# Attention, a cosine gate and a second expert in one kernel: the first two token blocks share the loading of the weights

## The chip, the cores and the metric

The kernel runs on one core of one Trainium2 chip, as a single launch. The metric is the device time of that launch in microseconds. Three runs of the kernel before took 1356.47, 1359.84 and 1358.34 us, so the median is 1358.34 us. A profiled execution, from which all rows below come, took 1353.98 us.

## The reference

Three stages follow each other. The first is an attention with pooled keys and values; its output is the input of a two-matrix stage with the gate h * cos(h); that output goes through a second two-matrix stage with a softmax-weighted gate and a layer norm. All arithmetic is float32.

```python
# q, k, v: (8, 8, 576, 64)
k_p = k.reshape(B, H, 72, 8, D).mean(axis=3)
v_p = v.reshape(B, H, 72, 8, D).mean(axis=3)
scores = scale * q @ k_p.T
attn = softmax(scores)
x = (attn @ v_p) -> (4608, 512)

h = x @ w_in                 # (4608, 2048)
y = (h * cos(h)) @ w_out     # (4608, 512)

h2 = y @ w2_in               # (4608, 1024)
solu = h2 * softmax(h2)
out = (layernorm(solu) * g_ln) @ w2_out
```

The matrices w_in, w_out, w2_in, w2_out arrive as float64 bits and are turned into float32 on the chip.

## The kernel before

The 4608 tokens are cut into 9 blocks of 512. The first part of the kernel, of which this document speaks, makes for every block the attention output x and from it h, in units. A unit is one block j and one pair q of 128-column chunks of w_in: 16 chunks make 8 pairs, so a block has 8 units and there are 72. A unit is 24 matmuls (`h_mm`, L608 to L622: two chunks, four row groups of x, and three products of high and low parts each) in 8 steps of three matmuls. The result stays in PSUM while a chain of four operations (`chain`, two on ScalarE (ACT), two on VectorE (DVE)) turns it into h * cos(h), which goes to DRAM. The later parts (y, and the second stage) read it from there, in an order of their own.

Around the units stand three kinds of other work, in an order that the program writes out by hand; each engine runs its own instructions in that order.

**Chunks of w_in.** Each of the 16 chunks is loaded as 64-bit words into a tile `raw` (L109, 512 KB), then goes through `s1` (ACT, L114 and L115), `bits` (DVE, L119, L123, L127), `join` (GpSimd (POOL), L139) and `c_in.done` (ACT L1100, POOL L1101), after which the chunk can be used in a matmul. The class `Pipe` moves three chunks at a time: each `pipe.step()` does bits and join of one chunk, the done of the one before and the s1 of the one after. Five steps stand before the units; in block 0 every unit has two more, at s = 1 and s = 5. Since ACT's s1 of a chunk takes a buffer that is freed by POOL's done of a chunk three earlier, the three engines go in step.

**Where chunks and other tiles lie.** Sixteen slots called `wi` hold the chunks for good. Before a chunk is there, a slot serves other tiles, given out in turn: slots 0 to 3 the raw keys of batch 0, 4 to 6 the v of batch 0 (`load_vn`), 7 to 9 the v of batch 1, 10 and 11 raw keys of batch 1, 12 the pooling matrix `pool_w`, 13 and 14 raw keys of batch 1. The raw words of chunks 6, 8, 10 and 12 to 15 are loaded into the chunk's own slot. So the load of chunk 8 goes into slot 8, which held the second tile of the v of batch 1, and the load of chunk 12 into that of `pool_w`; each must wait until the last pooling matmul that reads the old tile has run. All these loads and the loads of q (`load_q`, L379) stand in one queue, SP's, which issues in order.

**Attention of the next block.** For block 1 `Attn.plan` gives each piece a position, counted in steps of the units of block 0 (64 positions, 8 per unit): scores (`sc`, PE L391, then DVE L399 and L400, which free the PSUM tile), exponentials (ACT L457), `norm` (sums on DVE L476, scaling of the even heads of a pair on POOL and of the odd on DVE, L486 and L491), transposes (`eTp`, `eLp`, PE), their split in high and low parts (ACT, then DVE L527 and L510), and the products with v (`av`, PE L549, then ACT L551 and DVE L552), which write x. The score tiles, the transposes and the products all share two PSUM tiles, `ps_a`.

Block 0's attention stands before the units: keys of batch 0 are summed in groups of eight on DVE (L243, L245, L246), those of the other batches on POOL (L231, L251: `halves` and the last sum). The v of batches 0 and 1 is pooled by matmuls with `pool_w` (`pool_vn`, L287 and L290, two halves each) and brought into shape by `prep_vn` (DVE L301, L308, L317, ACT L314, L315, POOL L316).

Of the kernel before, what the change touches and what calls it, by code (L numbers as in the profile page):

```python
# [11 lines left out]
F32 = mybir.dt.float32  # L12
# [23 lines left out]
def fused_kernel(ctx, tc, qT_d, kT_d, vN_d, vM_d, vL_d, w_in, w_out, w2_in, w2_out, g_ln, out):  # L36
# [184 lines left out]
    def kv_jobs(b, hf):  # L221


        def raw_tile(n):
            if b < 2:
                return wi.tile([P, n], F32, "kvraw")
            return wo.tile([P, n], F32, "kvraw")

        def halves(x, n):
            for m in (4 * n, 2 * n):  # L230
                nc.gpsimd.tensor_tensor(out=x[:, 0:m], in0=x[:, 0:m], in1=x[:, m:2 * m], op=ALU.add)  # L231
            return x

        def k_job(i):
            p = 2 * hf + i
            raw = raw_tile(POOL * SP)
            nc.sync.dma_start(out=raw, in_=kT_d[b, p])
            dst = kT[b % 2][p]

            def add():  # L240
                if b == 0:
                    t = wo.tile([P, SP], F32, "kp")
                    nc.vector.tensor_reduce(  # L243
                        out=t, in_=raw.rearrange("p (r s) -> p s r", r=POOL), axis=AX.X, op=ALU.add)
                    nc.vector.tensor_copy(out=dst[0:D, 0:SP], in_=t[0:D])  # L245
                    nc.vector.tensor_copy(out=dst[D:P, SP:2 * SP], in_=t[D:P])  # L246
                else:
                    x = halves(raw, SP)
                    for a in range(2):
                        r = slice(D * a, D * (a + 1))  # L250
                        nc.gpsimd.tensor_tensor(  # L251
                            out=dst[r, SP * a:SP * (a + 1)], in0=x[r, 0:SP], in1=x[r, SP:2 * SP],
                            op=ALU.add)
            return add

        def v_job(i):
            if hf == 0 and i == 0:
                v_t[b] = ap1.tile([P, 6, D], F32, tag="v", name="v")
            dst = v_t[b][:, 2 * hf + i if i < 2 else 4 + hf]
            raw = raw_tile(POOL * D)  # L260
            nc.sync.dma_start(out=raw, in_=vM_d[b - 2, 2 * hf + i] if i < 2 else vL_d[b - 2, hf])

            def add():
                x = halves(raw, D)
                nc.gpsimd.tensor_tensor(out=dst, in0=x[:, 0:D], in1=x[:, D:2 * D], op=ALU.add)
            return add

        n = 3 if b >= 2 else 0
        return [lambda i=i: k_job(i) for i in range(2)] + [lambda i=i: v_job(i) for i in range(n)]
# [8 lines left out]
        nc.sync.dma_start(out=t[2][0:64, 0], in_=vN_d[b, 4, 0:64])  # L278

    def pool_vn(b, hf):  # L280
        if hf == 0:
            pool_vn.ps = ps_y.tile([P, 2, BLK], F32, tag="y", name="vps")
        main, left = pool_vn.ps[:, 0], pool_vn.ps[:, 1]
        t = v_t[b]
        c = slice(4 * D * hf, 4 * D * (hf + 1))
        for i in range(4):
            nc.tensor.matmul(  # L287
                main[:, c], lhsT=pool_w["m"][:, i], rhs=t[i // 2][:, i % 2, c], start=(i == 0),
                stop=(i == 3))
        nc.tensor.matmul(  # L290
            left[:, c], lhsT=pool_w["l"][0:64], rhs=t[2][0:64, 0, c], start=True, stop=True)
        v_t[b, hf] = main, left

    def prep_vn(b, hf):
        main, left = v_t.pop((b, hf))
        vm, vl = vM[b][:, hf], vL[b][:, hf]
        c = slice(4 * D * hf, 4 * D * (hf + 1))
        w = wo.tile([P, 4 * D], F32, "vw")
        u = wo.tile([P, 2, 4 * D], F32, "vu")
        hi = wo.tile([P, 4 * D], F32R, "vh")  # L300
        nc.vector.tensor_tensor(  # L301
            out=w.rearrange("p (i a d) -> p i a d", i=2, a=2),
            in0=main[:, c].rearrange("p (i a d) -> p i a d", i=2, a=2),
            in1=m_half.rearrange("p (o a u) -> p o a u", o=1, u=1).to_broadcast([P, 2, 2, D]),
            op=ALU.mult,
        )
        for k2, m in enumerate((m_head, m_hlo)):
            nc.vector.tensor_tensor(  # L308
                out=u[:, k2].rearrange("p (c d) -> p c d", c=4),
                in0=left[:, c].rearrange("p (c d) -> p c d", c=4),  # L310
                in1=m.rearrange("p (c o) -> p c o", o=1).to_broadcast([P, 4, D]), op=ALU.mult,
            )
        w = w.rearrange("p (i c) -> p i c", i=2)
        nc.scalar.copy(out=vm[:, 0], in_=w)  # L314
        nc.scalar.copy(out=hi, in_=u[:, 0])  # L315
        nc.gpsimd.tensor_tensor(out=vm[:, 1], in0=w, in1=vm[:, 0].bitcast(F32), op=ALU.subtract)  # L316
        nc.vector.scalar_tensor_tensor(  # L317
            out=vl.rearrange("p i c -> p (i c)"), in0=hi.bitcast(F32), scalar=m_sh, in1=u[:, 1],
            op0=ALU.mult, op1=ALU.add)

    def prep_v(b):
        src = v_t.pop(b)
# [34 lines left out]
    class Attn:  # L357
# [101 lines left out]
        def norm(self, *ps):  # L459
# [22 lines left out]
            def scale():  # L482
                for i, (p, e) in enumerate(zip(ps, es)):
                    i2 = p % 2
                    eng = nc.vector if self.j < 2 and i2 else nc.gpsimd
                    eng.tensor_tensor(  # L486
                        out=em[:, :, i2], in0=e[:, :, :, 0:KM],
                        in1=sv[:, i].to_broadcast([P, TPB, 2, KM]), op=ALU.mult,
                    )
                    for a in range(2):  # L490
                        eng.tensor_tensor(  # L491
                            out=el[:, :, 2 * i2 + a],
                            in0=e[:, :, a:a + 1, KM:SP].to_broadcast([P, TPB, 4, KL]),
                            in1=sv[:, i, :, a:a + 1].to_broadcast([P, TPB, 4, KL]), op=ALU.mult,
                        )
# [17 lines left out]

        def e_tr(self, p):
            hf, i2 = divmod(p, 2)
            tp = ps_a.tile([P, BLK], F32, tag="a", name="eTp")
            em = self.em[hf]
            eT = self.eT[p] = self.tile([P, 2, BLK], F32R, "eT")

# [39 lines left out]
        def plan(self, put):  # L559
# [29 lines left out]
            if self.j == 1:  # L589
                for i in range(2):  # L590
                    put(i, add, 1, 1, KV[i])
            for b in new:
                for i in range(6):
                    put(-10 + 2 * i, kv_load, b, i // 3, KV[2 + i % 3])
                    put(2 * i + i // 3, add, b, i // 3, KV[2 + i % 3])
# [4 lines left out]

    NQ = NF // 2
    units = [(j, q) for j in range(NB) for q in range(NQ)]
    yd = [dram.tile([P, KD, BLK], F32, tag="yd", name=f"yd{j}") for j in range(NB)]
    gd = [dram.tile([P, NQ, 2, BLK], F32, tag="gd", name=f"gd{j}") for j in range(NB)]
    w_in_t, w_op = [], [{} for _ in range(NQ)]
# [3 lines left out]
        return t.rearrange("p a b -> p (a b)")  # L609

    def h_mm(n, i, kk):
        j, q = units[n]
        if i == 0 and kk == 0:
            pool, tag = ((ps_q, "q"), (ps_y, "y"), (ps_y, "y"))[n % 3]
            h_ps[n] = pool.tile([P, 2, BLK], F32, tag=tag, name="h")
# [23 lines left out]
            h_ps.pop(n)  # L639

    def g_store(n):
        j, q = units[n]
        nc.sync.dma_start(out=gd[j][:, q], in_=h_t.pop(n))

    NH = BLK // 2
# [447 lines left out]
    def c_in(f):  # L1093
# [20 lines left out]
    with tc.manual_schedule():  # L1114
# [4 lines left out]
        for p in range(NPAIR):  # L1119
            kv_load(0, p // 2, KV[p % 2])  # L1120
            a0.load_q(p)
            if p == 1:
                order[0].load(raws[0])
        load_vn(0)
        for i in (1, 2, 3):
            order[i].load(raws[i])
# [44 lines left out]
        nc.scalar.activation(out=cst[:, 36:37], in_=halfpi, func=AF.Exp)  # L1171
        add(0, 0, "k0", "k1")
        a0.scores0(0)
        add(0, 1, "k0")
        a0.scores0(1)
        pipe.step()
        a0.now("norm", 0)
        add(0, 1, "k1")
        a0.scores0(2)
        a0.scores0(3)  # L1180
        a0.now("norm", 1)
        pipe.step()
        pool_vn(0, 0)
        pool_vn(0, 1)
        prep_vn(0, 0)
        a0.now("e_tr", 0)
        a0.now("norm", 2)
        a0.now("norm", 3)
        a0.now("e_tr_left", 0)
        a0.now("e_tr", 1)  # L1190
        prep_vn(0, 1)
        a0.now("av", 0)
        a0.now("e_tr", 2)
        add(1, 0, "k1")
        a0.now("av", 1)
        pipe.step()
        pool_vn(1, 0)
        a0.now("e_tr", 3)
        add(1, 0, "k0")
        a0.now("e_tr_left", 1)  # L1200
        prep_vn(1, 0)
        a0.now("av", 2)
        pool_vn(1, 1)
        pipe.step()
        prep_vn(1, 1)
        a0.now("av", 3)
        early = {7: raws[1], 9: raws[2], 11: raws[3]}
        pipe.todo += [(order[i], early.get(i)) for i in range(6, len(order))]
        pipe.step()
# [7 lines left out]
                work[BL * (j - 1) + pos].append(lambda: fn(*a))  # L1217
            return put

        for j in range(1, NB):  # L1220
            at[j].plan(put_at(j))
        last = len(units) - 1
        raws = [ap1.tile([P, BLK, 2], I32, tag=t, name="raw") for t in ("em", "eT")]
# [19 lines left out]
            put(50 + 7 * m, g_split, m)  # L1243
        put(62, g_load, 2)
        for n in range(len(units)):
            j, q = units[n]
            for s in range(SL):
                h_mm(n, s // KD, s % KD)
                if n > 1 and s == 3:
# [2 lines left out]
                    chain(n - 1, (0, 4, 7).index(s))  # L1252
                if n > 1 and s == 5:
                    g_store(n - 2)
                if j == 0 and s in (1, 5):
                    pipe.step()
                for fn in work[SL * n + s]:
                    fn()
# [200 lines left out]
```

## Time and profile before

| | us |
|---|---|
| three runs | 1356.47, 1359.84, 1358.34 |
| profiled execution | 1353.98 |
| its span | 1352.2 |
| PE busy | 1300.9 (96%) |
| DVE busy | 1059.3 (78%) |
| ACT busy | 697.7 (52%) |
| POOL busy | 499.8 (37%) |

The span is the time from the first to the last instruction; the execution's own time is 1.8 us longer. Shares are averages over stages: PE is busy for 96% of the whole, and what is left idle lies mostly in the first 100 us and around 550 us. PE's matmuls, its weight loads (PEld) and the other engines are listed apart, SPq is the DMA queue of SyncE.

### The profile page before, as it was taken

To read this page: it belongs to the slowest core of one execution; us is meant where nothing else is said; L and a number is where in the kernel's file an instruction comes from. 1 tells how busy PE (TensorE), PEld (TensorE's weight loads), DVE (VectorE), ACT (ScalarE), POOL (GpSimd) and SP (SyncE) were. 2 spreads that over 40 slices of the span, in tenths; PEclk is the share of its full clock that TensorE was granted. 3 is DMA by queue.
4 is the path that set the end of the run, shared out by engine and by line. 5 is a ranking of instruction groups with operands and counts; after the bars stand their busy time and mean duration, and the time that the engine had idled before them with its cause. 6 is when DMAs were issued, how large, how long until landed. Compare 5 with 4: busy or idle time off the path is not lost. (4 is left out here: it accounts for less than half of the span.)

```text
span 1352.2 us, 20435 instructions
## 1 busy us (share of the span) xinstructions
PE 1300.9 (96%) x7510; PEld 1133.5 (84%) x7510; DVE 1059.3 (78%) x1686; ACT 697.7 (52%) x992; POOL 499.8 (37%) x668
## 2 busy tenths in 40 slices
PE   5779999999999999889999999999999999999998
PEld 4558877887887888789999999999878888888887
DVE  7897887978879684688889999895777767676753
ACT  5576666756557466544444444444444444444432
POOL 3868676665554125330110101001343434343410
PEclk8989999999999999999999999999999999999999
DMA  8425566664655526454555555558511111111101
GB/s 296 155 82 200 190 239 236 235 244 160 238 210 187 187 109 233 173 198 136 149 153 169 165 170 172 154 183 304 200 33 55 40 55 40 55 40 55 40 24 39
DMA packets 81268, 202.93 MB, mean 150 GB/s; under 512 B 7824, under 2 KB 26256, under 8 KB 81168
## 3 DMA queue, kind: packets, MB, share of 16 engines
q1 hardware_dynamic: 81024, 201.62, 44.2%
q8 instruction: 59, 0.97, 0.3%
q14 instruction: 41, 0.34, 0.1%
q10 hardware_dynamic: 144, 0.00, 0.0%
HBM read 124.00 MB, written 77.59 MB: 149 GB/s over the span
## 5 line engine op out<-in xcount | busy, mean ns | idle before, releaser
L619 PE MATMUL h<-x,w 128*128 128x512 f32 x1728 | 436.1, 401 | 1.9 <-DVE t L638 1.9
L701 PE MATMUL y<-g,wy 128*128 128x256 f32 x3024 | 367.6, 284 | 7.4 <-DVE g L677 3.8
L701 PEld LDWEIGHTS y<-g,wy 128*128 128x128 f32 x3024 | 366.1, 193 | 9.1 <-DVE g L677 4.7
L619 PEld LDWEIGHTS h<-x,w 128*128 128x128 f32 x1728 | 317.9, 190 | 66.5 <-issue 3.2
L675 ACT CAST g<-gs 128x1024 fp32r<-128x1024 f32 x72 | 75.8, 1052 | 175.8 <-PE y L701 93.7
L636 ACT ACTIVATE t<-t,cst 128x1024 f32<-128x1024 f32 x72 | 82.9, 1152 | 65.6 <-DVE t L633 65.5
L677 DVE TENSOR_TENSOR g<-gs,g 128x1024 fp32r<-128x1024 f32 x72 | 90.3, 1254 | 30.3 <-ACT g L675 29.9
L139 POOL TENSOR_TENSOR dec<-dec,raw 128x512 int32<-128x512 int32 x24 | 34.0, 1416 | 209.2 <-DVE dec L127 175.4
L638 DVE TENSOR_TENSOR t<-t,h 128x1024 f32<-128x1024 f32 x72 | 87.4, 1214 | 25.9 <-ACT t L636 25.9
L901 POOL TENSOR_TENSOR yl<-yr,yh 128x1024 fp32r<-128x1024 f32 x18 | 43.3, 2408 | 153.6 <-ACT yh L896 153.6
L630 ACT ACTIVATE t<-h 128x1024 int32<-128x1024 f32 x72 | 73.4, 1019 | 47.3 <-PE h L619 46.6
L633 DVE SCALAR_TENSOR_TENSOR t<-t,h 128x1024 f32<-128x1024 int32 x72 | 87.3, 1213 | 4.0 <-ACT t L630 4.0
L231 POOL TENSOR_TENSOR kvraw<-kvraw 128x256 f32<-128x256 f32 (+3 forms) x128 | 82.9, 648 | 7.8 <-DMA kvraw<-in_vL 1.3
L664 DVE TENSOR_TENSOR gs<-gr,gs 128x256 f32<-128x256 f32 x144 | 72.1, 501 | 5.0
L677 DVE TENSOR_TENSOR g<-gr,g 128x768 fp32r<-128x768 f32 x72 | 75.1, 1043 | 0.0
L1032 POOL TENSOR_TENSOR sc<-sc,cst 128x1 f32<-128x1 f32 x36 | 20.3, 565 | 141.1 <-DVE sc L1021 113.7
L1067 ACT COPY o<-o 128x512 f32<-128x512 f32 x36 | 21.1, 587 | 96.7 <-PE o L1085 96.7
L1083 PE MATMUL o<-w,lh 128*128 128x512 f32 x176 | 69.0, 392 | 0.0
L1085 PE MATMUL o<-w,ll 128*128 128x512 f32 x176 | 68.5, 389 | 0.0
L1084 PE MATMUL o<-w,lh 128*128 128x512 f32 x176 | 68.5, 389 | 0.0
L164 POOL TENSOR_TENSOR wy<-ws,wy 128x512 fp32r<-128x512 f32 (+1 forms) x32 | 40.0, 1283 | 63.4 <-ACT wy L163 63.1
L139 POOL TENSOR_TENSOR wf<-dec,raw 128x512 int32<-128x512 int32 x24 | 31.4, 1307 | 84.7 <-DVE dec L127 48.0
(179 smaller groups left out, 2557.4 us busy)
## 6 DMA issues: line engine op xcount, KB each, us to landing
gd<-t SPq DMA_DIRECT2D x72, 512.0 KB, 2.9
gr<-gd SPq DMA_DIRECT2D x72, 512.0 KB, 4.0
raw<-in_w_in SPq DMA_DIRECT2D x24, 512.0 KB, 5.0
raw<-in_w_out SPq DMA_DIRECT2D x24, 512.0 KB, 4.9
kvraw<-in_kT SPq DMA_DIRECT2D x32, 288.0 KB, 4.1
qT<-in_qT SPq DMA_DIRECT2D x36, 256.0 KB, 4.5
yd<-yo SPq DMA_DIRECT2D x36, 256.0 KB, 4.6
yr<-yd SPq DMA_DIRECT2D x18, 512.0 KB, 3.9
```

What stands on the lines that cost most here:

```text
L231: nc.gpsimd.tensor_tensor(out=x[:, 0:m], in0=x[:, 0:m], in1=x[:, m:2 * m], op=ALU.add)
L619: nc.tensor.matmul(h_ps[n][:, i], lhsT=w[:, a, kk, :], rhs=x[:, b], start=(kk == 0 and m == 0), stop=(kk == KD - 1 and m == 2),)
L630: nc.scalar.activation(out=t.bitcast(I32), in_=h, func=AF.Copy, scale=1.0 / TWO_PI, bias=0.25)
L633: nc.vector.scalar_tensor_tensor(out=t, in0=t.bitcast(I32), scalar=-TWO_PI, in1=h, op0=ALU.mult, op1=ALU.add)
L636: nc.scalar.activation(out=t, in_=t, func=AF.Sin, bias=halfpi)
L638: nc.vector.tensor_tensor(out=t, in0=t, in1=h, op=ALU.mult)
L664: nc.vector.tensor_tensor(out=o, in0=x, in1=y, op=ALU.subtract)
L675: nc.scalar.copy(out=flat(g[-1])[:, 0:n * NH], in_=flat(f)[:, 0:n * NH])
L677: nc.vector.tensor_tensor(out=flat(g[-1])[:, 0:n * NH], in0=flat(f)[:, 0:n * NH], in1=flat(g[-2])[:, 0:n * NH].bitcast(F32), op=ALU.subtract)
L701: nc.tensor.matmul(y_ps[j][i][:, NH * c:NH * (c + 1)], lhsT=w[:, a, P * c:P * (c + 1)], rhs=g[y][b], start=(q == 0 and c == 0 and k == 0), ...
L1083: nc.tensor.matmul(ps, lhsT=hi, rhs=w[:, 0], start=(c == 0), stop=False)
L1084: nc.tensor.matmul(ps, lhsT=hi, rhs=w[:, 1], start=False, stop=False)
```

## The change

Units are put in a new order: block 0's first five pairs, block 1's first five, block 0's last three, block 1's last three, and then the other blocks as before. So the chunks 10 to 15 are first used in unit 10 instead of unit 5, and block 1's attention must be done by unit 5 instead of unit 8. Its positions are multiplied by 5/8. The pipe steps once in every unit while chunks are left, and a second time in units 0 to 3.

Four pieces of work change engine or place: the odd key tiles of batch 0 are summed on POOL instead of DVE; in block 1 the odd heads are scaled on POOL too; the v of batch 1 is pooled and prepared within units 0 and 1 and uses the `ps_a` tiles; the raw words of chunk 0 are loaded behind all keys and queries of block 0. The order of block 0's attention is written anew, and its middle two transposes use a tile of `ps_y`.

```diff
@@ kv_jobs / k_job
-                if b == 0:
+                if b == 0 and i == 0:
                     t = wo.tile([P, SP], F32, "kp")
...
@@ pool_vn
+        if b > 0:
+            ps = ps_a.tile([P, 2, 4 * D], F32, tag="a", name="vps")
+            main, left = ps[:, 0], ps[:, 1]
+        else:
+            if hf == 0:
+                pool_vn.ps = ps_y.tile([P, 2, BLK], F32, tag="y", name="vps")
+            main, left = pool_vn.ps[:, 0, c], pool_vn.ps[:, 1, c]
...
@@ prep_vn: the same instructions, now in three functions
+        def first():
...
+        def second():
...
+        def third():
...
+        return first, second, third
@@ Attn.norm / scale
-                    eng = nc.vector if self.j < 2 and i2 else nc.gpsimd
+                    eng = nc.vector if self.j == 0 and i2 else nc.gpsimd
@@ Attn.e_tr
-            tp = ps_a.tile([P, BLK], F32, tag="a", name="eTp")
+            if self.j == 0 and p in (1, 2):
+                if p == 1:
+                    self.tp = ps_y.tile([P, 2, BLK], F32, tag="y", name="eTp")
+                tp = self.tp[:, p - 1]
+            else:
+                tp = ps_a.tile([P, BLK], F32, tag="a", name="eTp")
@@ Attn.plan
             if self.j == 1:
                 for i in range(2):
                     put(i, add, 1, 1, KV[i])
+                    put(2 + 7 * i, pool_vn, 1, i)
+                    staged((5 + 7 * i, 7 + 7 * i, 10 + 7 * i), prep_vn, 1, i)
@@ units
+    Q0 = 5
+    units_h = [(j, q) for part in (range(Q0), range(Q0, NQ)) for j in (0, 1) for q in part]
+    units_h += units[2 * NQ:]
@@ h_mm, g_store
-        j, q = units[n]
+        j, q = units_h[n]
@@ loads before the units
-            if p == 1:
-                order[0].load(raws[0])
+        order[0].load(raws[0])
@@ block 0's attention, written anew (two lines of it)
-        add(0, 1, "k0")
+        add(0, 1, "k0", "k1")
...
@@ plan of block 1
-        for j in range(1, NB):
+        at[1].plan(lambda pos, fn, *a: put_at(1)(max(0, pos * Q0 // NQ), fn, *a))
+        for j in range(2, NB):
             at[j].plan(put_at(j))
@@ the loop over units
-                if j == 0 and s in (1, 5):
+                if s == 1 and pipe.busy or s == 5 and n < Q0 - 1:
                     pipe.step()
```

On PE, at the start of the units, the program before has the following rows: vps is the pooling of v (here of batch 1), xo the product with v of block 0, h a unit, sc block 1's scores.

```order
L549 MATMUL xo<-eL,vL_100 128x512
L287 MATMUL vps<-vn,pool_w 128x256 x4
L290 MATMUL vps<-vn,pool_w 128x256
L549 MATMUL xo<-eT,vM_98 128x512 x3
L549 MATMUL xo<-eL,vL_100 128x512
L619 MATMUL h<-x,w 128x512 x3
L391 MATMUL sc<-kT_90,qT 64x144
L391 MATMUL sc<-kT_94,qT 64x144
L391 MATMUL sc<-kT_94,qT 128x144
L619 MATMUL h<-x,w 128x512 x9
L391 MATMUL sc<-kT_94,qT 128x144 x2
L619 MATMUL h<-x,w 128x512 x9
```

In the changed program PE has there, from the first unit to the scores of the third pair of heads (kT_92):

```order
L639 MATMUL h<-x,w 128x512 x3
...
L401 MATMUL sc<-kT_94,qT 128x144 x2
L291 MATMUL vps<-vn,pool_w 128x256 x4
L294 MATMUL vps<-vn,pool_w 128x256
L639 MATMUL h<-x,w 128x512 x6
L401 MATMUL sc<-kT_91,qT 64x144
...
L401 MATMUL sc<-kT_95,qT 128x144 x2
L291 MATMUL vps<-vn,pool_w 128x256 x4
L294 MATMUL vps<-vn,pool_w 128x256
L639 MATMUL h<-x,w 128x512 x6
L401 MATMUL sc<-kT_92,qT 64x144
```

Both poolings of batch 1's v now stand between the units' matmuls, the second directly ahead of the third pair's scores, and the scores follow each other after 6 matmuls instead of 9.

On POOL, before, the sums of batch 1's first keys (L231 and L251) stand on either side of chunk 1's join and chunk 0's done:

```order
L231 TENSOR_TENSOR kvraw<-kvraw 128x288
L231 TENSOR_TENSOR kvraw<-kvraw 128x144
L251 TENSOR_TENSOR kT_95<-kvraw 64x72 x2
L139 TENSOR_TENSOR dec<-dec,raw_163 128x512
L1101 TENSOR_TENSOR w<-dec,w 128x512
L231 TENSOR_TENSOR kvraw<-kvraw 128x288
L231 TENSOR_TENSOR kvraw<-kvraw 128x144
L251 TENSOR_TENSOR kT_94<-kvraw 64x72 x2
L316 TENSOR_TENSOR vM_99<-vw,vM_99 128x256
L139 TENSOR_TENSOR dec<-dec,raw_164 128x512
L1101 TENSOR_TENSOR w<-dec,w 128x512
```

In the changed program both pairs of sums stand behind them, and directly ahead of chunk 2's join and chunk 1's done:

```order
L139 TENSOR_TENSOR dec<-dec,raw_163 128x512
L1121 TENSOR_TENSOR w<-dec,w 128x512
L231 TENSOR_TENSOR kvraw<-kvraw 128x288
L231 TENSOR_TENSOR kvraw<-kvraw 128x144
L251 TENSOR_TENSOR kT_95<-kvraw 64x72 x2
L231 TENSOR_TENSOR kvraw<-kvraw 128x288
L231 TENSOR_TENSOR kvraw<-kvraw 128x144
L251 TENSOR_TENSOR kT_94<-kvraw 64x72 x2
L139 TENSOR_TENSOR dec<-dec,raw_164 128x512
L1121 TENSOR_TENSOR w<-dec,w 128x512
```

SP's queue at this place has the same order in both programs; here it is in the changed one, from chunk 5 (raw0) on. raw_516 is chunk 8, whose slot held the v of batch 1, raw_555 chunk 12, and qT_566 the queries of block 1's third pair of heads:

```order
L109 DMA raw0_162<-in_w_in 128x1024
L109 DMA raw_513<-in_w_in 128x1024
L109 DMA raw1_163<-in_w_in 128x1024
L109 DMA raw_516<-in_w_in 128x1024
L109 DMA raw2_164<-in_w_in 128x1024
L109 DMA raw_519<-in_w_in 128x1024
L109 DMA raw3_165<-in_w_in 128x1024
L109 DMA raw_555<-in_w_in 128x1024
L389 DMA qT_566<-in_qT 128x512
```

What has moved is the place of the pooling matmuls for which raw_516 waits: before the units in the program before, within unit 0 in the changed one.

## Rows read from the trace of the kernel before

**Rows 1.** The page's first part: busy time, share of the span, instructions.

```profile
PE 1300.9 (96%) x7510; PEld 1133.5 (84%) x7510; DVE 1059.3 (78%) x1686; ACT 697.7 (52%) x992; POOL 499.8 (37%) x668
```

**Rows 2.** Busy time of each engine in stretches of the span; granted clock, DMA last.

```profile
core 0: us, PE busy (x) PEld busy (x) DVE busy (x) ACT busy (x) POOL busy (x), PEclk, DMA share, GB/s
0.00:43.00 43.00, 27.82 (x112) 21.08 (x113) 34.44 (x84) 22.32 (x76) 17.34 (x38) 0.88 0.72 247
43.00:121.40 78.40, 63.12 (x290) 49.55 (x289) 67.72 (x97) 49.31 (x72) 59.63 (x66) 0.93 0.41 141
62.50:99.00 36.50, 26.47 (x109) 20.13 (x107) 35.74 (x54) 27.86 (x41) 22.20 (x21) 0.86 0.23 81
...
121.40:146.00 24.60, 24.60 (x126) 20.82 (x125) 22.10 (x37) 17.69 (x23) 15.92 (x24) 1.00 0.50 175
```

**Rows 3.** Instructions in order of time: start, duration (us), engine, line, operation.

```profile
44.30 0.69 DVE L552 TENSOR_TENSOR x<-xo,x 128x512 fp32r<-128x512 f32 x1
...
45.53 0.67 ACT L114 ACTIVATE dec<-raw 128x512 f32<-128x512 f32 x1 [0.73 <-POOL w L1101]
...
49.78 0.42 SPq L379 DMA_DIRECT2D qT<-in_qT  x1
...
50.77 0.44 DVE L399 TENSOR_REDUCE mx<-sc 128x4 f32<-128x288 f32 x1
...
59.49 0.91 PE L391 MATMUL sc<-kT,qT 128*64 128x144 f32 x6 [2.09 <-issue]
...
115.11 6.98 PE L619 MATMUL h<-x,w 128*128 128x512 f32 x30
```

**Rows 4.** DVE's groups from 0 to 43 us: count, busy us, mean ns.

```profile
L243 DVE TENSOR_REDUCE kp<-kvraw 128x72 f32<-128x576 f32 x4 | 4.7, 1180 | 0.3 <-DMA kvraw<-in_kT 0.2
...
L308 DVE TENSOR_TENSOR vu<-vps,cst 128x256 f32<-128x256 f32 x7 | 2.6, 412 | 0.0
L486 DVE TENSOR_TENSOR em<-e,sm 128x512 f32<-128x512 f32 x2 | 2.1, 1054 | 0.1
```

**Rows 5.** POOL's groups from 43 to 99 us.

```profile
L139 POOL TENSOR_TENSOR dec<-dec,raw 128x512 int32<-128x512 int32 x12 | 16.0, 1333 | 16.7 <-DVE dec L127 13.4 <-ACT t L630 2.0 <-issue 1.1
L1101 POOL TENSOR_TENSOR w<-dec,w 128x512 fp32r<-128x512 f32 x11 | 15.2, 1384 | 0.0
L486 POOL TENSOR_TENSOR em<-e,sm 128x512 f32<-128x512 f32 x2 | 2.6, 1301 | 0.0
L231 POOL TENSOR_TENSOR kvraw<-kvraw 128x288 f32<-128x288 f32 x2 | 2.1, 1028 | 0.0
L251 POOL TENSOR_TENSOR kT<-kvraw 64x72 f32<-64x72 f32 x4 | 1.9, 475 | 0.3
```

**Rows 6.** DVE's groups from 43 to 99 us.

```profile
L127 DVE SCALAR_TENSOR_TENSOR dec<-raw,dec 128x512 int32<-128x512 int32 x11 | 8.6, 782 | 0.4
L119 DVE TENSOR_SCALAR dec<-dec 128x512 f32<-128x512 f32 x12 | 8.1, 679 | 3.0 <-ACT dec L114 3.0
L123 DVE TENSOR_SCALAR dec<-dec 128x512 int32<-128x512 int32 x11 | 7.3, 668 | 0.4
...
L491 DVE TENSOR_TENSOR el<-e,sm 128x128 f32<-128x128 f32 x4 | 4.0, 1027 | 0.0
...
L486 DVE TENSOR_TENSOR em<-e,sm 128x512 f32<-128x512 f32 x2 | 3.0, 1494 | 0.0
```

**Rows 7.** PE's groups from 0 to 43 us.

```profile
L287 PE MATMUL vps<-vn,pool_w 128*128 128x256 f32 x32 | 8.8, 422 | 0.5 <-DVE vu L308 0.5
...
L290 PE MATMUL vps<-vn,pool_w 64*128 64x256 f32 x8 | 2.8, 428 | 0.0
```

**Rows 8.** What SP's queue waited for from 20 to 62 us: total, times, longest.

```profile
SPq L109 <- PE vps L287: 3.9, 1, 3.9
```

**Rows 9.** DMA: GB/s in 40 slices of 0 to 45 us; issues of 43 to 52 us.

```profile
GB/s 0 57 305 389 244 401 390 403 408 395 388 255 260 397 411 395 381 388 227 283 388 411 391 406 397 386 98 18 15 0 0 0 0 22 262 182 0 51 302 113
...
qT<-in_qT SPq DMA_DIRECT2D x1, 256.0 KB, 4.5
```

More of the change, by code (lines that the diff above doesn't have):

```diff
@@ L280, in pool_vn @@
     def pool_vn(b, hf):
-        if hf == 0:
-            pool_vn.ps = ps_y.tile([P, 2, BLK], F32, tag="y", name="vps")
-        main, left = pool_vn.ps[:, 0], pool_vn.ps[:, 1]
         t = v_t[b]
         c = slice(4 * D * hf, 4 * D * (hf + 1))
+        if b > 0:
[5 more added lines that the diff above has]
+            main, left = pool_vn.ps[:, 0, c], pool_vn.ps[:, 1, c]
         for i in range(4):
             nc.tensor.matmul(
-                main[:, c], lhsT=pool_w["m"][:, i], rhs=t[i // 2][:, i % 2, c], start=(i == 0),
+                main, lhsT=pool_w["m"][:, i], rhs=t[i // 2][:, i % 2, c], start=(i == 0),
                 stop=(i == 3))
         nc.tensor.matmul(
-            left[:, c], lhsT=pool_w["l"][0:64], rhs=t[2][0:64, 0, c], start=True, stop=True)
+            left, lhsT=pool_w["l"][0:64], rhs=t[2][0:64, 0, c], start=True, stop=True)
         v_t[b, hf] = main, left
@@ L296, in prep_vn @@
         vm, vl = vM[b][:, hf], vL[b][:, hf]
-        c = slice(4 * D * hf, 4 * D * (hf + 1))
         w = wo.tile([P, 4 * D], F32, "vw")
@@ L300, in prep_vn @@
         hi = wo.tile([P, 4 * D], F32R, "vh")
[L301 to L307, printed above, removed]
+        w2 = w.rearrange("p (i c) -> p i c", i=2)
+        def first():
             nc.vector.tensor_tensor(
-                out=u[:, k2].rearrange("p (c d) -> p c d", c=4),
-                in0=left[:, c].rearrange("p (c d) -> p c d", c=4),
-                in1=m.rearrange("p (c o) -> p c o", o=1).to_broadcast([P, 4, D]), op=ALU.mult,
-            )
[L313 to L319, printed above, removed]
+                out=w.rearrange("p (i a d) -> p i a d", i=2, a=2),
+                in0=main.rearrange("p (i a d) -> p i a d", i=2, a=2),
+                in1=m_half.rearrange("p (o a u) -> p o a u", o=1, u=1).to_broadcast([P, 2, 2, D]),
+                op=ALU.mult,
+            )
+            for k2, m in enumerate((m_head, m_hlo)):
+                nc.vector.tensor_tensor(
+                    out=u[:, k2].rearrange("p (c d) -> p c d", c=4),
+                    in0=left.rearrange("p (c d) -> p c d", c=4),
+                    in1=m.rearrange("p (c o) -> p c o", o=1).to_broadcast([P, 4, D]), op=ALU.mult,
+                )
+        def second():
+            nc.scalar.copy(out=vm[:, 0], in_=w2)
+            nc.scalar.copy(out=hi, in_=u[:, 0])
+        def third():
+            nc.gpsimd.tensor_tensor(out=vm[:, 1], in0=w2, in1=vm[:, 0].bitcast(F32), op=ALU.subtract)
+            nc.vector.scalar_tensor_tensor(
+                out=vl.rearrange("p i c -> p (i c)"), in0=hi.bitcast(F32), scalar=m_sh, in1=u[:, 1],
+                op0=ALU.mult, op1=ALU.add)
+        return first, second, third
     def prep_v(b):
@@ L641, in g_store @@
     def g_store(n):
-        j, q = units[n]
+        j, q = units_h[n]
         nc.sync.dma_start(out=gd[j][:, q], in_=h_t.pop(n))
@@ L1103, in c_in, with now @@
         return Chunk(w_in_w[f], done, home)
+    def now(fns):
+        for fn in fns:
+            fn()
     def kv_load(b, hf, *names):
@@ L1173, in fused_kernel @@
         a0.scores0(0)
-        add(0, 1, "k0")
+        add(0, 1, "k0", "k1")
         a0.scores0(1)
-        pipe.step()
         a0.now("norm", 0)
-        add(0, 1, "k1")
         a0.scores0(2)
         a0.scores0(3)
+        pipe.step()
         a0.now("norm", 1)
-        pipe.step()
+        a0.now("e_tr", 0)
         pool_vn(0, 0)
-        pool_vn(0, 1)
-        prep_vn(0, 0)
-        a0.now("e_tr", 0)
+        now(prep_vn(0, 0))
         a0.now("norm", 2)
-        a0.now("norm", 3)
         a0.now("e_tr_left", 0)
         a0.now("e_tr", 1)
-        prep_vn(0, 1)
+        pool_vn(0, 1)
+        a0.now("norm", 3)
+        pipe.step()
+        a0.now("e_tr", 2)
         a0.now("av", 0)
-        a0.now("e_tr", 2)
+        now(prep_vn(0, 1))
+        a0.now("av", 1)
+        a0.now("e_tr", 3)
+        a0.now("e_tr_left", 1)
+        pipe.step()
         add(1, 0, "k1")
-        a0.now("av", 1)
+        a0.now("av", 2)
+        add(1, 0, "k0")
+        a0.now("av", 3)
         pipe.step()
[L1197 to L1206, printed above, removed]
         early = {7: raws[1], 9: raws[2], 11: raws[3]}
@@ L1245, in fused_kernel @@
         for n in range(len(units)):
-            j, q = units[n]
             for s in range(SL):
```

## The prediction

> **What bounds the kernel now.** I read the page's busy shares first, then the stretches, then the order of time at the start of the units, then the queue of loads. PE is busy for 96% of the span [rows 1], and from 121.4 us on, when unit 8 begins, it is busy without a break (24.60 of 24.60 us) [rows 2]. So an edit pays only by what unit 8 begins earlier, and nothing in the diff touches what follows: the rest moves along. Unit 8 begins at 121.4 us because the last run of matmuls of block 0 and 1 starts at 115.11, takes 6.98 us for 30 (0.233 each), and 27 of them are block 0's [rows 3].
>
> Ahead of that lie 43.0 us before the units, in which PE works 27.8, and 78.4 us of units, in which it works 63.1, idles 15.3, and has a granted clock of 0.93 [rows 2]. Between 62.5 and 99 us DVE is busy for 35.7 of 36.5 us and PE for 26.5: there DVE is the bound [rows 2]. About 15 us, and what the head can give, are all there is to win.
>
> **The change, by four moments.** I follow the moments that pass on the delay, with the durations of before, each instruction starting when its engine is free and what it needs is there.
>
> *End of the head.* x of the last pair is written at 44.30 + 0.69 = 45.0 [rows 3]. Out go two key sums on DVE (1.18 us each, with two short copies 1.6) [rows 4] and two v preparations (four instructions of about 0.41 us each, 1.65) [rows 4], 6.5 us of DVE, and from PE two poolings. One pooling is 8.8 / 4 + 2.8 / 4 = 2.9 us [rows 7]. Not all of it is on the path: the product with v, its copy and its split wait for each other as before, and the odd products now wait for the even ones' split. The gain lies between 0 and 6.9 us; stepping through the new order I get x at 40.4, a gain of 4.6, which is nearer the upper end. The keys on POOL cost nothing there: POOL works 17.3 of the 43 us [rows 2], and the load of chunk 0, now behind the keys, hides them.
>
> *The first score reduction of block 1*, at 50.77 [rows 3]. On DVE it stands behind the bits of chunk 4, these wait for ACT's s1, and that for POOL's done of chunk 1: the row of 45.53 shows ACT let go by just that line [rows 3]. In front of this done POOL now has batch 1's first keys. From the end of chunk 1's bits (36.0, which is 4.4 before x): join and done 1.33 + 1.38, two key sums of 1.03 + half of it + 2 x 0.475, 2.5 each, again join and done, is 2.7 + 5.0 + 2.7 [rows 5], so 46.4. Then 0.67 for s1 and 0.68 + 0.67 + 0.78 = 2.1 for the bits [rows 3, 6]: 49.2. Of the 4.6 us, 1.6 are left.
>
> *The third pair's scores*, at 59.49 [rows 3]. Now PE must first pool v twice, in `ps_a` tiles: the first pooling waits for the reduction and its subtraction (50.1), ends at 53.0; 12 matmuls of a unit and the two score tiles follow (3.1 + 1.6), and the second pooling's reads end 2.2 later, at 59.9. Only then may SP load chunk 8 over the v it replaces. The program before has that wait too, 3.9 us long [rows 8], but ahead of the units, and the queries of the third pair, which stand in SP's queue five loads later, were issued at 49.78 [rows 3], ten us before their use. In the changed program they are issued two us after 59.9, with 5 x 0.524 + 0.262 = 2.88 MB in the queue. At the head's 0.40 MB per us [rows 9] that is 7.2 us. The single issue of 49.78 took 4.5 us for its own 0.26 MB behind one chunk [rows 9], 2 us more than that rate gives; so 9.2, and the queries are there at 69.1. The lower end is 2.2 + 4.5 = 6.7. I take 9.2, because five loads are let go at once. PE would have been ready at 59.9 + 0.7 + 1.6 = 62.2, so it stands for 6.9 us, DVE and ACT behind it too, since their next instructions need the same scores. This moment is 9.6 us later than before.
>
> *From there to unit 8*, 61.9 us before. PE's work in the units is 63.1 + 5.8 for the poolings; 24 matmuls (5.6), four score tiles (some 0.8 each, 3.1) and the poolings (5.8) are done, so 54.4 remain and, without any wait, unit 8 begins at 123.5. Block 1's attention must now come out beside 3.5 units rather than 6.5: counted over the new order with the rows' durations, DVE has some 36 us of work from those scores to block 1's last x, and PE 36 as well. Where two queues are equally long, each waits for the other now and then. The bounds are 0 and the 15.3 us that PE idled before [rows 2]; since DVE gives up em and el (3.0 + 4.0 us) [rows 6] and units 5 to 7 have almost nothing beside them, I take 3.2, nearer zero. Unit 8 at 126.7, which is 5.3 us later.
>
> In one sum: -4.6 (head) + 3.0 (POOL's keys) + 11.2 (poolings and the queries' wait) - 4.3 (denser units) = +5.3. The profiled execution, 1353.98 us, becomes 1359.3; on the median of the runs, 1358.34, that is 1363.6.
>
> **A rule against the odd keys on POOL.** In the head, where POOL is mostly idle, DVE's em took 1.05 us on average [rows 4], in the units 1.49 [rows 6], while POOL's own took 1.30 beside it [rows 5]. The Trainium skill (SBUF — State Buffer, "Who interferes with whom") says that a DVE instruction with two SBUF inputs and a GpSimd instruction that reads SBUF hold one port by turns, the loser blocked for the whole instruction; the trace agrees. By that rule the 7.0 us that leave DVE come back as waits of its other instructions.
>
> **Rivals.** *The wait turns into a gain (faster).* Its place is the third pair's scores again: if the queries land before PE gets there (62.2), nothing stands. This asks for a landing 2.3 us after the release, half of what one issue took, or for a release at about 55 us, should the pooling come earlier because the head gains more than 6.9. For it speaks that DVE was the bound from 62.5 to 99 and loses 7.0 of its 35.7 us. PE then ends at 62.2 + 54.4 = 116.6; with 0.5 to 2 us of waits unit 8 comes 2.8 to 4.3 us early, and with the head's full gain 6: a median of 1354 (1352 to 1355.5). Against it speaks the queue.
>
> *Gains and losses cancel (same).* The landing takes 6.7 us after the release, and afterwards PE never waits: 66.6 + 54.4 = 121.0, 0.4 early, 1358.
>
> *POOL becomes the bound (slower still).* From 38 us to block 1's last x it has 12 chunks of 2.7, four key sums of batch 1 and four of batch 2 (20), four em of 1.3 with their el (9) and v: 63 us in about 67, where it had 59.6 in 78.4 [rows 2, 5]. If DVE's two-input instructions then wait for it as the em did, the 7 us come back: 1370.
>
> **How the numbers follow.** Forecast 0.44, with its own range 1360 to 1368; faster rival 0.20; cancelling 0.24; POOL's bound 0.12. A measurement of this kernel tells about 0.3% from no change, 4.1 us: 1354.3 to 1362.4. Of the forecast's 0.44 a quarter lies below 1362.4. So slower 0.33 + 0.12 = 0.45, same 0.11 + 0.24 = 0.35, faster 0.20. The range runs from 1352.5, into the faster rival, to 1370.
>
> **What would show it.** In the profile after: x of the last pair at about 40 us; the first score reduction of block 1 at 49 and not below 46; in SP's queue a wait of the chunk loads for the pooling until about 60 us; PE idle for 5 to 7 us in front of the third pair's scores, with a wait for the queries; then PE nearly without gaps until unit 8 at 125 to 128. Wrong would be a start of those scores at about 62 with no gap, or a DVE that is again 98% busy behind it.

## The result, and the profile after

The changed kernel takes 1364.76 us (median of 5 runs, 1362.92 to 1366.92) against 1357.69 us (1354.43 to 1359.84) for the kernel before on the same chip: a ratio of 1.0055, 95% interval 1.0036 to 1.0075. It is 7.1 us slower; 5.3 were forecast, as a median of 1363.6. Its profiled execution took 1362.92 us with a span of 1361.1, 8.9 more than the span before.

| moment (us) | before | forecast | after |
|---|---|---|---|
| x of the last pair of block 0 written | 45.0 | 40.4 | 38.1 |
| first score reduction of block 1 | 50.8 | 49.2 | 49.5 |
| third pair's scores | 59.5 | 69.1 | 70.4 |
| unit 8 begins | 121.4 | 126.7 | 126.5 |

The stretches of the changed kernel (start:end, length; busy us of PE, PEld, DVE, ACT and POOL with counts; granted clock, DMA share, GB/s), to be read against [rows 2]:

```profile
0.00:36.60 36.60, 21.66 (x92) 16.70 (x93) 27.48 (x69) 19.76 (x71) 14.55 (x36) 0.95 0.78 273
36.60:63.00 26.40, 18.46 (x65) 12.23 (x63) 16.26 (x30) 8.37 (x15) 21.16 (x26) 0.74 0.10 30
63.00:72.00 9.00, 1.65 (x8) 1.22 (x8) 1.11 (x3) 7.29 (x12) 3.24 (x3) 0.75 1.02 402
72.00:100.00 28.00, 25.00 (x125) 19.82 (x125) 27.23 (x43) 18.57 (x27) 20.44 (x24) 0.96 0.31 110
100.00:126.00 26.00, 24.98 (x113) 20.12 (x112) 20.35 (x26) 16.66 (x23) 20.44 (x24) 1.00 0.32 113
```

The units now begin at 36.6 us, and 9 us are nearly empty: from 63 to 72 us PE works 1.65, DVE 1.11, and the DMA engines run full at 402 GB/s, after having been at a tenth of their time for 26 us. Behind that PE is busy for 50.0 of 54 us. In order of time (start, duration, engine, line, operation; in brackets what ended the wait), to [rows 3]:

```profile
37.43 0.69 DVE L567 TENSOR_TENSOR x<-xo,x 128x512 fp32r<-128x512 f32 x1 [1.91 <-ACT x L566]
37.49 1.45 POOL L231 TENSOR_TENSOR kvraw<-kvraw 128x288 f32<-128x288 f32 x2
...
41.80 1.05 POOL L251 TENSOR_TENSOR kT<-kvraw 64x72 f32<-64x72 f32 x2
42.90 1.52 PE L401 MATMUL sc<-kT,qT 128*64 128x144 f32 x4 [3.84 <-POOL kT L251]
44.16 1.28 POOL L1121 TENSOR_TENSOR w<-dec,w 128x512 fp32r<-128x512 f32 x1
45.48 0.67 ACT L114 ACTIVATE dec<-raw 128x512 f32<-128x512 f32 x1 [0.61 <-POOL w L1121]
47.02 1.37 DVE L123 TENSOR_SCALAR dec<-dec 128x512 int32<-128x512 int32 x1
49.51 0.45 DVE L409 TENSOR_REDUCE mx<-sc 128x4 f32<-128x288 f32 x1
50.60 3.61 PE L291 MATMUL vps<-vn,pool_w 128*128 128x256 f32 x8 [3.94 <-DVE e L410]
56.33 0.43 DVE L123 TENSOR_SCALAR dec<-dec 128x512 int32<-128x512 int32 x1
58.98 1.89 PE L291 MATMUL vps<-vn,pool_w 128*128 128x256 f32 x8
60.80 0.70 PE L294 MATMUL vps<-vn,pool_w 64*128 64x256 f32 x2
63.49 0.43 SPq L389 DMA_DIRECT2D qT<-in_qT  x1
70.43 1.53 PE L401 MATMUL sc<-kT,qT 128*64 128x144 f32 x6 [7.35 <-DMA qT<-in_qT]
127.00 0.65 PE L401 MATMUL sc<-kT,qT 128*128 128x144 f32 x4
```

The second pooling's eight main matmuls end at 58.98 + 1.89 = 60.87. SP issues the first chunk load that waited for them at 60.90, four more follow, and the queries of the third pair are issued at 63.49. PE, which had stood for 7.35 us, starts on them at 70.43. Until 60.90 SP's queue had stood; its wait for the pooling (total, times, longest) was 3.9 us in [rows 8] and is now

```profile
SPq L109 <- PE vps L291: 24.2, 1, 24.2
```

The last row of time above is block 2's first scores, 0.53 us behind the start of unit 8 in every kernel here (121.93 before). In the experiments unit 8 is read from it.

### The profile page after: what moved, and what is told of

Read it like the earlier page. It is cut to its first block, busy times and chain, and to the rows that moved or that the text cites. A ratio compares the mean times of both kernels' runs of the same rounds, so it can differ in the third digit from the quotient of the medians.

```text
span 1361.1 us, 20441 instructions
## 1 busy us (share of the span) xinstructions
PE 1303.0 (96%) x7510; PEld 1134.1 (83%) x7510; DVE 1051.6 (77%) x1674; ACT 697.3 (51%) x992; POOL 506.5 (37%) x682
## 5 line engine op out<-in xcount | busy, mean ns | idle before, releaser
L231 POOL TENSOR_TENSOR kvraw<-kvraw 128x128 f32<-128x128 f32 (+3 forms) x132 | 85.6, 648 | 11.2 <-DMA kvraw<-in_kT 2.5
L139 POOL TENSOR_TENSOR wf<-dec,raw 128x512 int32<-128x512 int32 x24 | 31.4, 1310 | 81.1 <-DVE dec L127 47.2
```

## The experiments

Runs of one kernel lie up to 10 us apart (before: 1353.7 to 1360.8 over all of them), and the experiments ran on different chips, so times are compared by their ratio to before on the same chip. Moments are read from one profiled run of each kernel. How far such runs differ shows where two kernels have the same head: before and with the odd heads on POOL, x of the last pair is written 2.2 us apart.

| kernel | median us | ratio, 95% interval | unit 8 |
|---|---|---|---|
| changed | 1364.76 | 1.0055 (1.0036 to 1.0075) | 126.5 |
| queries early | 1358.87 | 1.0014 (1.0000 to 1.0028) | 119.3 |
| poolings ahead | 1355.44 | 0.9989 (0.9978 to 1.0000) | 118.1 |
| keys first | 1366.32 | 1.0071 (1.0059 to 1.0084) | 126.7 |
| odd heads on DVE | 1368.61 | 1.0087 (1.0071 to 1.0103) | 129.2 |
| eight pairs | 1361.72 | 1.0043 (1.0031 to 1.0055) | 126.6 |
| old head | 1364.95 | 1.0045 (1.0024 to 1.0066) | 125.4 |
| before + odd heads on POOL | 1357.77 | 0.9999 (0.9987 to 1.0011) | 122.3 |
| poolings ahead, keys first | 1354.55 | 0.9991 (0.9981 to 1.0000) | 117.6 |
| ... and steps behind | 1352.62 | 0.9975 (0.9962 to 0.9988) | 116.3 |
| ... and queries early | 1355.51 | 0.9989 (0.9976 to 1.0002) | 116.0 |
| ... steps behind, eight pairs | 1355.26 | 0.9988 (0.9976 to 1.0000) | 122.3 |

**Queries early.**

```diff
-                if self.j > 1 or p > 1:
+                if self.j > 1:
                     put(-10 + 6 * p, self.load_q, p)
...
+        at[1].load_q(2)
+        at[1].load_q(3)
         early = {7: raws[1], 9: raws[2], 11: raws[3]}
```

> The changed kernel, with block 1's queries of pairs 2 and 3 loaded ahead of the chunk loads that wait for the v pooling. Theory (the queries' wait is on the path): PE's 7.35 us in front of the third pair's scores go, these start at about 63 instead of 70.4, and since PE and DVE have the same work behind them, unit 8 begins 5 to 7 us earlier than in the changed kernel (119 to 121.5 instead of 126.5): a median of 1357.5 to 1360. Rival (POOL or the shared port is the bound behind 72 us, so the time comes back as DVE waits): the scores start at 63 as well, but unit 8 moves by less than 3 us, 1362 or more.

PE, in order of time:

```profile
61.06 1.65 PE L639 MATMUL h<-x,w 128*128 128x512 f32 x6
62.64 0.91 PE L401 MATMUL sc<-kT,qT 128*64 128x144 f32 x6
119.79 0.65 PE L401 MATMUL sc<-kT,qT 128*128 128x144 f32 x4
```

The scores follow the unit's matmuls without a gap, and unit 8 is 7.2 us earlier, the whole wait. The chunk loads wait as long as before (24.0 us), so it was the queries behind them that cost, not the late chunks. The rival falls.

**Poolings ahead.** Both poolings stand before the units, the preparations behind the next step:

```diff
-                    put(2 + 7 * i, pool_vn, 1, i)
-                    staged((5 + 7 * i, 7 + 7 * i, 10 + 7 * i), prep_vn, 1, i)
...
         a0.now("av", 3)
+        pool_vn(1, 0)
+        pool_vn(1, 1)
         pipe.step()
+        now(prep_vn(1, 0))
+        now(prep_vn(1, 1))
```

> The changed kernel, with both poolings of batch 1's v ahead of the units again, right behind the last product of the head, in tiles of the same kind. Theory: PE stood there for 3.84 us anyway, waiting for POOL's keys, and for 3.94 us before the first pooling, so the 5.8 us of matmuls are nearly free; the v tiles are read by about 43 instead of 61.5, the loads are let go by POOL's bits of chunk 7 (48) instead, the queries land at 53 to 57.5, and the third pair's scores start at 56 to 58. Unit 8 begins 8 to 13 us earlier than in the changed kernel (113.5 to 118.5), a median of 1352 to 1357. Rival (DVE or POOL is the bound of the units, whatever the queries do): the scores start at 57, and unit 8 is within 4 us of 126.5, 1361 or more.

```profile
36.75 3.46 PE L291 MATMUL vps<-vn,pool_w 128*128 128x256 f32 x8
42.77 0.70 PE L294 MATMUL vps<-vn,pool_w 64*128 64x256 f32 x2
44.29 0.91 PE L401 MATMUL sc<-kT,qT 128*64 128x144 f32 x6
58.77 0.91 PE L401 MATMUL sc<-kT,qT 128*64 128x144 f32 x6
118.59 0.65 PE L401 MATMUL sc<-kT,qT 128*128 128x144 f32 x4
```

The matmuls that the change moved into the units cost little in front of them: the scores that waited for POOL's keys until 42.90 run at 44.29. The third pair's scores come 11.7 us earlier, a little later than expected, and unit 8 8.4 us. This undoes the loss: by the ratios, 0.9989 against 1.0055, it is about 9 us faster than the changed kernel.

**Keys first.** Batch 1's first keys move on POOL from behind to ahead of chunk 1's join, by moving two lines:

```diff
         now(prep_vn(0, 1))
+        add(1, 0, "k1", "k0")
...
-        add(1, 0, "k1")
         a0.now("av", 2)
-        add(1, 0, "k0")
```

> The changed kernel, with batch 1's first keys on POOL ahead of the join of chunk 1, in the 3.9 us in which POOL waited for DVE (31.1 to 35.0), instead of behind it. Theory: chunk 0's weights come 1 us later, chunk 1's 4 us earlier (41.2 instead of 45.4), the first score reduction of block 1 at about 45.5 instead of 49.5, the first pooling, the release of the loads and the queries move with it, and so does unit 8: about 122.5, a median of 1359 to 1362. Rival (that moment was not on the path; the queue of loads takes its own time): the reduction comes at 45.5, the queries still land at about 70, and the time is that of the changed kernel, 1363.5 to 1366.

```profile
47.12 0.45 DVE L409 TENSOR_REDUCE mx<-sc 128x4 f32<-128x288 f32 x1
```

```profile
48.21 3.75 PE L291 MATMUL vps<-vn,pool_w 128*128 128x256 f32 x8 [7.03 <-DVE e L410]
53.04 2.93 PE L639 MATMUL h<-x,w 128*128 128x512 f32 x6
58.91 1.89 PE L291 MATMUL vps<-vn,pool_w 128*128 128x256 f32 x8
70.58 1.52 PE L401 MATMUL sc<-kT,qT 128*64 128x144 f32 x6 [7.57 <-DMA qT<-in_qT]
```

My theory fell. The rival's time nearly held (1366.32 against at most 1366), for a reason that neither had. The reduction came 2.4 us earlier (4 were expected), the first pooling too, and the second pooling stood where it had been, at 58.91. PE's pause ahead of the first had grown from 3.94 to 7.03 us, and what follows ran at half clock (stretch; PE's busy time; granted clock):

```profile
41.20:48.20 7.00, 0.00 (x0) 0.64 0.00 1
48.20:56.90 8.70, 8.69 (x21) 0.50 0.00 0
56.90:62.90 6.00, 6.00 (x28) 1.00 0.18 49
```

In the changed kernel it was near half for the pooling alone:

```profile
50.60:54.70 4.10, 4.10 (x10) 0.59 0.00 0
54.70:62.90 8.20, 8.20 (x39) 1.00 0.12 28
```

From the first pooling to the second it is 10.70 us here and 8.38 there, with PE busy throughout both: 2.3 of the 2.4 us were given back to the clock. The Trainium skill (TensorE: Matmul & The Clock Gate, Part 1) says that PE falls to 1.2 of its 2.4 GHz when it idles; the rows agree.

**Odd heads on DVE.** `eng = nc.vector if self.j < 2 and i2 else nc.gpsimd`, as before the change.

> The changed kernel, with the odd heads' scales (em, el) of block 1 on DVE again, all else kept. Theory (DVE is the bound from 72 to 100 us, 27.2 of 28.0 us busy, and what left it was a gain): 7 us more on DVE there, unit 8 is 3 to 7 us later than in the changed kernel, 1367.5 to 1372. Rival (port: what left DVE came back as its waits, or the queue of POOL's em, el is on the path): the same or faster, 1361 to 1366, and DVE's mean durations of two-input instructions in that stretch fall when POOL does less.

Unit 8 came 2.7 us later, a little less than expected, and by the ratios the time rose by 4.3 us, with intervals that just overlap. The rival needed DVE's bits to become shorter; from 72 to 100 us none did by more than 6% (with the odd heads on DVE L123 takes 0.67 us against 0.66 in the changed kernel, L127 0.69 against 0.73). POOL's idle time ahead of the joins (columns: count, busy us, mean ns, idle us and what ended it) doubles. Of the 5.2 us more, 1.7 ended with DVE's bits and 3.0 with a matmul. The changed kernel, then this one, 72 to 100 us:

```profile
L139 POOL TENSOR_TENSOR dec<-dec,raw 128x512 int32<-128x512 int32 x4 | 5.2, 1304 | 4.5 <-DVE dec L127 3.7 <-DMA kvraw<-in_kT 0.8
```

```profile
L139 POOL TENSOR_TENSOR dec<-dec,raw 128x512 int32<-128x512 int32 x4 | 5.2, 1296 | 9.7 <-DVE dec L127 5.4 <-PE h L639 3.0 <-ACT w L1120 1.2
```

**Before, with the odd heads on POOL alone.** The same line in the kernel before: `if self.j == 0 and i2`.

> The kernel before, with one part of the change alone: the odd heads' scales (em, el) of block 1 on GpSimd. Theory (DVE was the bound from 62.5 to 99 us, 35.7 of 36.5 us busy, and the 7.0 us that leave it are what shortened the units): unit 8 begins 3 to 6 us earlier than before (115.5 to 118.5), a median of 1351 to 1354. Rival (shared port, or POOL's longer queue: the 7 us come back as waits): unit 8 within 1.5 us of 121.4, 1355.5 to 1358.5.

The rival held: no change. This profile's head ran 2.2 us later than that of [rows 3] (x of the last pair at 47.2), so unit 8 at 122.3 is 75.1 us behind x instead of 76.4; 1.3 us came through. Between these two moments DVE was busy for 63.7 us, against 65.9 before: of the 7.0 us that left it, 4.9 came back. The bits of the chunks, 72 to 100 us, before and with the part:

```profile
L123 DVE TENSOR_SCALAR dec<-dec 128x512 int32<-128x512 int32 x6 | 3.6, 603 | 0.2
L127 DVE SCALAR_TENSOR_TENSOR dec<-raw,dec 128x512 int32<-128x512 int32 x5 | 3.5, 692 | 0.2
```

```profile
L123 DVE TENSOR_SCALAR dec<-dec 128x512 int32<-128x512 int32 x5 | 5.1, 1022 | 0.2
L127 DVE SCALAR_TENSOR_TENSOR dec<-raw,dec 128x512 int32<-128x512 int32 x5 | 4.3, 852 | 0.2
```

The instructions that stayed on DVE became longer: 0.6 us more per chunk in these two lines. In the denser units of the changed kernel the same lines took 0.66 and 0.73 us, and there the move was worth something. The scales themselves cost DVE less there: 3.3 us in the run with the odd heads on DVE, instead of 7.0.

**Eight pairs.** `Q0 = 8` instead of 5 in the changed kernel.

> The changed kernel with eight instead of five f pairs of block 0 ahead of block 1's first (each block's eight pairs in one piece, as before the change), all else kept. Theory (the denser units are worth 4.3 us, as the prediction's sum has it): block 1's attention is spread over eight units again, unit 8 comes 3 to 5 us later than in the changed kernel (129.5 to 131.5), a median of 1367.5 to 1370. Rival (what shortened the units is what left DVE, not the split into five and three; PE's idle time behind the third pair's scores was only 4 us anyway): the queries' wait stays at 6 to 8 us, unit 8 within 2 us of 126.5, 1363 to 1366.5.

```profile
60.10 2.34 PE L639 MATMUL h<-x,w 128*128 128x512 f32 x9
69.35 1.52 PE L401 MATMUL sc<-kT,qT 128*64 128x144 f32 x6 [6.91 <-DMA qT<-in_qT]
127.13 0.65 PE L401 MATMUL sc<-kT,qT 128*128 128x144 f32 x4
```

The rival held on unit 8, which begins at 126.6, as with five pairs. At the third pair's scores, which come 1.1 us earlier, PE has here done 39 of the units' matmuls instead of 24 (3.5 us). It loses both behind them, to waits and to a lower granted clock (0.87 from 72 to 100 us, against 0.96). By the ratios the time was 1.6 us better than the changed kernel's, which the overlapping intervals don't show to be a gain. A difference of 1.4 us does lie behind unit 8: from 128 to 200 us PE idles 0.6 us in every kernel with eight pairs and 2.0 to 2.1 in every one with five. Block 2's first transposes, in the kernel before and in the changed one:

```profile
149.88 0.66 PE L522 MATMUL eTp<-ident,em 128*128 128x128 f32 x4 [0.18 <-DVE eT L527]
```

```profile
156.35 0.66 PE L537 MATMUL eTp<-ident,em 128*128 128x128 f32 x4 [1.57 <-DVE eT L542]
```

What in the five-pair order sets this wait was not settled.

**Old head.** The changed kernel with the head of before: its order, the odd keys of batch 0 summed on DVE, no transposes in a tile of `ps_y`. The v of batch 1 stays in the units. Some of the lines:

```diff
-                if b == 0 and i == 0:
+                if b == 0:
...
         pipe.step()
-        a0.now("norm", 1)
+        pool_vn(0, 0)
+        pool_vn(0, 1)
+        now(prep_vn(0, 0))
         a0.now("e_tr", 0)
...
+        a0.now("e_tr", 2)
+        add(1, 0, "k1")
+        a0.now("av", 1)
         pipe.step()
...
```

> The changed kernel with the head in the order of before (odd keys of batch 0 summed on DVE, both poolings of v of batch 0 first, a transpose tile of its own kind), v of batch 1 still in the units. Theory (of the head's gain most was lost at POOL's chunk 1 and the queries): x of the last pair at 41 to 43.5 instead of 38.1, the first score reduction at 49.5 to 51.5, unit 8 up to 2 us later than in the changed kernel, a median of 1364 to 1367. Rival (the head's gain passes through in full): unit 8 3 to 5.5 us later, 1367.5 to 1371.

```profile
40.60 0.69 DVE L567 TENSOR_TENSOR x<-xo,x 128x512 fp32r<-128x512 f32 x1 [0.97 <-ACT x L566]
47.29 0.44 DVE L409 TENSOR_REDUCE mx<-sc 128x4 f32<-128x288 f32 x1
```

x comes 3.2 us later, and the first reduction 2.2 us earlier, where I expected it no earlier; unit 8 is 1.1 us earlier. In this order POOL makes one of batch 1's two key tiles at 28.6 to 31.0, when it would stand idle. Its next join begins at 34.69, in the changed kernel at 35.00, so the new head had not brought it forward; and chunk 1's done begins at 41.16 instead of 44.16. So nothing of the new head's gain reached the units. The runs spread widely (1358.38 to 1367.60), and the time is not to be told from the changed kernel's.

**Poolings ahead and keys first.** Both of these edits together.

> Both poolings of batch 1's v ahead of the units, and batch 1's first keys on POOL ahead of the join of chunk 1. Theory (with the release of the loads out of the way, the earlier keys pass on): the first score reduction at 48.5 to 49.5 instead of 51.3, the third pair's scores at 55 to 57 instead of 58.8, unit 8 at 115.5 to 117, a median of 1352 to 1354. Rival (PE's pause ahead of its next matmuls grows by what is gained, and the granted clock falls, as with the keys moved alone): unit 8 at 118 and the time of the run with the poolings ahead alone, 1354.5 to 1357.

**... and steps behind.** In the loop over the units the pipe's step follows the slot's pieces:

```diff
+                for fn in work[SL * n + s]:
+                    fn()
                 if s == 1 and pipe.busy or s == 5 and n < Q0 - 1:
                     pipe.step()
-                for fn in work[SL * n + s]:
-                    fn()
```

> The run before (poolings ahead, keys first), and in each slot of a unit the step of the chunk pipeline behind the attention's pieces instead of ahead of them, so that the first score reduction no longer waits on DVE for the bits of chunk 4 (3.6 to 4.5 us of DVE, and ACT's wait for POOL ahead of them). Theory (what paces the first units is DVE's order): the first reduction at 44 to 46.5, PE's pause of 4.6 us ahead of the second pair's later scores shrinks to under 2, unit 8 1 to 3 us earlier than without it (113 to 116), a median of 1350 to 1353. Rival (POOL's chunks pace them, whatever stands first on DVE): the reduction comes earlier, unit 8 doesn't, 1353 to 1356.

**... and queries early.** The edit of the first experiment on top.

> The run before, and block 1's queries of pairs 2 and 3 ahead of the chunk loads. Theory (with the poolings ahead the queries land in time): no wait of PE for queries in either, the same time within 1.5 us. Rival (the queries are late again once all else is earlier): without this edit PE waits 1 to 3 us for them, with it the time falls by as much.

Keys first on top of the poolings gave 0.5 us at unit 8 and no difference in time that the intervals show, which is nearer to the rival. Steps behind brought the lowest median of all, 0.25% below before; its interval overlaps those of its neighbours in the table. In its rows PE waits 0.30 us instead of 3.61 ahead of the second pair's scores, but 2.08 us, where it had no wait, ahead of their second half:

```profile
49.58 0.91 PE L401 MATMUL sc<-kT,qT 128*64 128x144 f32 x6 [0.30 <-PE h L637]
53.96 1.20 PE L401 MATMUL sc<-kT,qT 128*128 128x144 f32 x4 [2.08 <-DVE e L410]
116.84 0.65 PE L401 MATMUL sc<-kT,qT 128*128 128x144 f32 x4
```

The first reduction, at 48.54, was later than I expected, in a profile whose x was 2.0 us later as well. With the queries early too unit 8 is the same within 0.3 us and no queries are waited for in either, as the theory said; the median lies 2.9 us higher, where 1.5 were allowed, and the intervals overlap, so that stays open.

**... steps behind, with eight pairs.**

> The best run so far (poolings ahead, keys first, steps behind), with eight f pairs instead of five ahead of block 1's first. Theory (the split into five and three gains nothing ahead of unit 8 and costs a wait of 1.6 us of PE behind it, as the run with eight pairs showed): unit 8 at 115 to 118 as without the edit, the wait behind it 0.2 us, a median of 1349 to 1352. Rival (with the front cleared the split does pay, since DVE has more to do per unit of PE): unit 8 at 118 or later, 1353 to 1356.

The numbers fall where the rival put them: with the front cleared and all eight pairs first, unit 8 begins 6.0 us later (122.3 against 116.3). But the profiled run is the slowest of this kernel's twelve (1359.71), and that of the run with the steps behind, 1351.18, one of its faster ones. By the ratios the difference is 1.8 us, and the intervals overlap. So that the split pays here is likely, and how much is not shown.

## Why the prediction was nearly right

*End of the head.* The gain was 6.9 us, the upper bound, not 4.6: x at 38.1. That fits removed work that had nearly all been on the path, but no run here takes the parts one by one, and the DVE work that the prediction names adds up to 6.5 us.

*The first score reduction.* 49.5 against 49.2, by the chain foretold: POOL made the keys until 42.85, then join and done, ACT was let go by L1121 at 45.48. Of the head's extra 2.3 us only 1.0 had reached POOL, whose join began at 35.00 instead of 36.0. One duration was off: the bits took 3.3 us instead of 2.1; they ran beside a working POOL (L123 1.37 us, L127 1.17; 0.43 and 0.69 at 56.33 to 57.48, with POOL idle). The Trainium skill (SBUF — State Buffer, "Who interferes with whom"), cited in the prediction for instructions with two inputs, as L127 is one, names a two-port mode as another case, which it says tensor_scalar can enter; L123 is a tensor_scalar with one input, but no run here shows its mode. So nothing was left of the head's larger gain.

*The third pair's scores.* 70.4 against 69.1. The loads were let go at 60.9 instead of 59.9, because the first pooling ran near half clock, 3.61 us instead of the 1.89 of the second. I had left out that PE's pause would lower the clock. From there to the scores it took 9.5 us, 9.2 were reckoned, and PE stood 7.35 (6.9). That this wait is the cause of the loss is shown twice: with the queries early it goes and unit 8 comes 7.2 us earlier; with the poolings ahead it goes and the kernel is no longer slower than before.

*From there to unit 8.* 56.1 us instead of 57.6, so the term was -5.8 instead of -4.3. The reason I gave was partly wrong. Denser units alone moved unit 8 by nothing in this kernel (eight pairs: 126.6), and what left DVE alone moved it by 1.3 us in the kernel before, where 4.9 of the 7.0 us came back, for the most part as the prediction's rule had it (its heading says odd keys; it is about the odd heads). In the changed kernel the move was worth 2.7 us. What the split adds once the front is cleared is not settled.

*What follows.* I took the rest to move along, and it did not quite: of the 8.9 us of span 5.1 stand at unit 8 and 3.8 come later, 1.4 of them in the wait of block 2's transposes, which the split brings. The others can't be told from the spread of the runs: from unit 8 to the end the profiled runs take 1230.8 us (before) to 1237.8 us (keys first), and even two kernels with the same order there, before and eight pairs, differ by 3.2.

The sum was -4.6 + 3.0 + 11.2 - 4.3 = +5.3; measured -6.9 + 5.6 + 12.2 - 5.8 = +5.1 at unit 8, plus 3.8. The signs and the main cost were right; that the sum came out so close is in part luck, since the errors of the terms, -2.3, +2.6, +1.0 and -1.5, nearly cancel. The rival with a gain failed where it had been put, at the landing of the queries. That of POOL as the bound did not come about, though DVE's bits took longer beside a working POOL.

## What to carry to other kernels

When work is moved, look up which buffers it reads and which load is to fill them next: the load then waits in its queue, and everything behind it too, though it needs none of those buffers. Loads that will be needed soonest belong ahead of any load that waits. A gain at the front is worth what the next things in line let through: here POOL's order, the clock behind a pause and the queue of loads each took it up.

## What the runs showed of the hardware

A gain ahead of a pause of PE can go to the clock: 2.4 us earlier, the pause 3.1 us longer, and 2.3 us lost at a granted clock of 0.50 (keys first). Work moved from DVE to POOL came back in good part as longer DVE instructions (in the kernel before with that part alone, 4.9 of 7.0 us; from 72 to 100 us L123 went from 603 to 1022 ns, L127 from 692 to 852). A load that waited for its buffer, for 24.2 us, held up the loads behind it in its queue: the queries, which needed no such buffer, were issued 2.6 us after its wait ended, and PE stood for 7.35 us.
